# Denominators turned by blocks and inverted by tokens, with a new order of ScalarE's copies and GpSimd's sums, in an mLSTM and gated-unit kernel

## The chip, the core and the metric

The kernel runs on one core of a Trainium2 chip. A core has TensorE (PE: matrix products, with its own queue of weight loads, PEld), VectorE (DVE), ScalarE (ACT), GpSimd (POOL) and SyncE (SP, whose queue starts most transfers). Each engine works through its own list of instructions in order, and they wait for each other by semaphores. The metric is the time of one execution on the device in microseconds (us), lower is better.

## The reference

Two blocks in a row, all in float32, except that `moe_w_in` and `moe_w_out` come as 64-bit floats, which the kernel turns into float32 itself.

```python
# block 1: mLSTM cell, B, H, S, D = 4, 8, 768, 40
for t in range(S):
    m_new = maximum(f_gate[t] + m, i_gate[t])
    f_stab, i_stab = exp(f_gate[t] + m - m_new), exp(i_gate[t] - m_new)
    C = f_stab * C + i_stab * outer(v[t], k[t])      # 40 x 40 for each batch and head
    n = f_stab * n + i_stab * k[t]
    denom = maximum(abs(n . q[t]), 1)
    y[t] = sigmoid(o_gate[t]) * (C @ q[t]) / denom
# block 2: x is (B*S, H*D) = (3072, 320); w_in is 320 x 2048, w_out 2048 x 320
h = x @ w_in
out = (h * cos(h)) @ w_out
```

What matters here is the last line of block 1: every head of every token has one denominator and one output gate for each of its 40 dimensions, and their quotient multiplies the head's vector.

## The kernel before, in words

The 768 tokens of a sequence are cut into six chunks of 128. A *cell* is one chunk of one batch element: cell n = 4c + b is chunk c of batch element b, 24 cells in all. The first four cells (chunk 0) are computed alone in `first_cells`. From then on each step of the program joins two kinds of work: block 2 for chunk c (`Up`, `sums`, `down_slot`) and block 1 for cell n = (c + 1) * 4 + b of the next chunk. `first_parts(b)` does this for c = 0 and `both_parts(c, b)` for c = 1 to 5; in c = 5 there are no cells left. Every such step has two halves, i = 0 and i = 1, and each half makes one pair of 128-wide slices of block 2's hidden layer, f2 = 2b + i.

The order is written out by hand (`tc.manual_schedule()`): the order of calls in the program is the order on each engine. So a call that is moved changes what an engine does first, and what is queued behind an instruction that waits.

**One half of block 2.** `Up` computes `pup` (two PSUM tiles) on TensorE from `xT` and the input weights. `near` (ScalarE) rounds to whole turns, `rest` (VectorE) takes the remainder, `sin` (ScalarE) the sine, `gate` (VectorE) multiplies into `g`. The two `pup` buffers come free when both gates are done. From chunk 1 on the down projection works on 2 x 2 blocks with seven products in place of eight, which needs sums of the gated values (`sums`: four VectorE instructions into `S`, and for c < 5 a GpSimd copy D for later) and sums of the weights (`weight_sums`: four GpSimd instructions, only during c = 0 and 1). TensorE takes those products from `all_products` in portions (`down_slot`, tile `acc`). Two of the seven, `late_products`, run in the next chunk's half f2 = 1. `combine_first`, `combine` and `combine_late` add the parts up to output rows: `m` is a ScalarE copy of an accumulator, `l` a ScalarE copy of the late products, and GpSimd adds `l` to the outputs.

**One cell of block 1.** From chunk 2 on (n >= TWO = 8) a cell is computed in two halves of 64 tokens with the state (`W`, tiles `two`) carried between them. `scores` makes the products of keys and queries and the state's increments, in two `ps` tiles (`pus` is their increment part). `weigh` multiplies by the decays (VectorE, `E<-ps` and `qG<-ps`), `state_half` adds an increment to the state (VectorE, `two<-two,ps`), `keep_end` copies the other increment to `ending` (ScalarE), `fade_end` and `fade_half` scale states (ScalarE, eight copies each), `add_end` adds `ending` to the state (GpSimd, two instructions), `decay_exponents` and `decay` make the next cell's decays (GpSimd, then ScalarE). `turn_blocks` turns the next cell's queries and keys in 32 x 32 blocks (VectorE, tiles `t`), `weigh_k` and `scale_q` weight keys and queries (GpSimd). `values` makes the heads in PSUM tile `vt`, transposed: 32 dimensions and 128 tokens per block of partitions, with the denominator in the row of one of the dimensions. The two `ps` tiles and `vt` share two PSUM buffers.

`turn_gate(n)` turns the output gates (`sig`, tile `og`: by tokens) into the transposed layout (`oT`), and `normalize_turned(n)` normalizes there, all on VectorE, lines 693 to 708: two bounds and a reciprocal over all 128 x 128 elements (of which the rows FROM0 and FROM1 of each block of 32 are denominators), three shuffles that spread them over the block, products with `oT`, and the product into `xT`, the input of block 2. The low dimensions take one more shuffle, one GpSimd product (L709) and two transfers on GpSimd's queue (`low_out`). In chunk 0 of the cells, `normalize` does the same by tokens.

## Time and profile before

| | |
|---|---|
| timed runs | 517.34, 518.75, 519.61 us; median 518.75 |
| the profiled execution | 516.43 us |
| its span, from the first to the last instruction | 514.7 us |
| TensorE's granted clock | 1.000 |
| TensorE busy | 494.4 us, 96% of the span |
| VectorE busy | 422.4 us, 82% |
| ScalarE busy | 350.0 us, 68% |
| GpSimd busy | 236.9 us, 46% |

Busy shares are averages over stages with different limits. A row of the timeline reads: start, duration, engine, source line, operation, output<-inputs, shape, count of merged instructions, and in brackets how long the engine was idle before it and what ended that. A row of a group reads: busy time, mean ns of one, idle time before, and what ended it. In the row of a stretch, each engine has its busy us and its count.

### The profile page before, as it was taken

How to read it: one execution, taken by the hardware profiler on the slowest of the kernel's cores; microseconds unless marked ns; L12 is line 12 of the kernel's file. 1: busy time of each engine (PE TensorE's matmuls, PEld its weight loads, DVE VectorE, ACT ScalarE, POOL GpSimd, SP SyncE). 2: the span in 40 equal slices, each digit the busy share in tenths (PEclk: the TensorE clock that was granted, in tenths of full speed). 3: DMA queues.
4: the chain of work that ended last, by engine and by line, in shares of the span. 5: the costliest groups of instructions: out<-in, count | busy, mean ns of one | idle time of the engine just before them, and what ended most of it. 6: DMA issues, size and time to landing. Idle time of an engine off the chain costs nothing.

```text
span 514.7 us, 12380 instructions
## 1 busy us (share of the span) xinstructions
PE 494.4 (96%) x4567; PEld 329.6 (64%) x4567; DVE 422.4 (82%) x965; ACT 350.0 (68%) x789; POOL 236.9 (46%) x383
## 2 busy tenths in 40 slices
PE   8989899999999999998999998999999999999996
PEld 5764455565565665675676676677676676666756
DVE  6687999987899999979889979889989888564536
ACT  5869897958878778778778787787866541322221
POOL 7626677645686686372462463453462341010000
PEclk9999999999999999999999999999999999999999
DMA  9997999989348156019647008838001000010001
GB/s 136 225 215 208 238 198 271 196 204 201 93 86 167 48 105 121 4 40 214 117 89 139 3 7 212 152 71 156 3 32 52 2 6 6 1 51 2 1 1 51
DMA packets 98092, 53.09 MB, mean 103 GB/s; under 512 B 63344, under 2 KB 90112, under 8 KB 98032
## 3 DMA queue, kind: packets, MB, share of 16 engines
q1 hardware_dynamic: 96176, 50.47, 47.1%
q0 software_dynamic: 1472, 1.48, 1.1%
q8 instruction: 36, 0.59, 0.5%
q10 hardware_dynamic: 384, 0.36, 0.2%
q14 instruction: 24, 0.20, 0.2%
HBM read 46.86 MB, written 4.11 MB: 99 GB/s over the span
## 4 chain that ended last, share of the span: by engine, by line
PE 56%; DVE 23%; ACT 9%; DMA 4%; issue 3%; POOL 3%; SPq 2%; ACTq 0%; DVEq 0%; POOLq 0%
PE pup L848 20%; PE acc L967 17%; PE pup L855 6%; PE po L887 3%; DVE g L875 3%; DVE n L866 3%; PE late L967 2%; PE vt L681 2%; DMA E<-M_d 2%; ACT two L759 2%; DVE E L624 1%; DVE t L563 1%; DVE qG L624 1%; ACT E L496 1%; DVE two L771 1%
## 5 line engine op out<-in xcount | busy, mean ns | idle before, releaser
L848 PE MATMUL pup<-xT,w_in_sb 128*128 128x512 f32 x384 | 176.0, 601 | 3.3 <-DVE g L875 2.5
L848 PEld LDWEIGHTS pup<-xT,w_in_sb 128*128 128x128 f32 x384 | 69.5, 190 | 90.1 <-issue 81.1
L863 ACT ACTIVATE n<-pup 128x512 int32<-128x512 f32 x96 | 53.5, 592 | 89.2 <-PE pup L855 51.4
L866 DVE SCALAR_TENSOR_TENSOR n<-pup,n 128x512 f32<-128x512 f32 x96 | 62.0, 684 | 54.0 <-ACT n L863 53.4
L871 ACT ACTIVATE n<-n 128x512 f32<-128x512 f32 x96 | 58.9, 630 | 25.2 <-DVE n L866 25.2
L759 ACT ACTIVATE two<-two,fades 40x48 f32<-40x48 f32 x224 | 64.0, 326 | 2.1
L875 DVE SCALAR_TENSOR_TENSOR g<-pup,n 128x512 f32<-128x512 f32 x96 | 61.9, 682 | 2.5
L967 PE MATMUL acc<-w_out_sb,g 128*128 128x160 f32 x320 | 58.6, 304 | 0.0
L967 PE MATMUL acc<-T,g 128*128 128x160 f32 x320 | 57.8, 300 | 0.0
L855 PE MATMUL pup<-xT,w_in_l 64*128 64x512 f32 (+1 forms) x256 | 54.0, 628 | 0.0
L967 PEld LDWEIGHTS acc<-w_out_sb,g 128*128 128x128 f32 x320 | 47.8, 190 | 4.7 <-issue 3.9
L967 PEld LDWEIGHTS acc<-T,g 128*128 128x128 f32 x320 | 48.2, 190 | 2.8 <-issue 2.7
L928 POOL COPY D<-S 128x256 f32<-128x256 f32 x32 | 12.7, 397 | 68.7 <-DVE S L924 68.7
L496 ACT ACTIVATE E<-E,tab 128x64 f32<-128x64 f32 (+1 forms) x160 | 42.1, 345 | 0.9 <-POOL E L482 0.7
L887 PE MATMUL po<-w_out_sb,g 128*128 128x320 f32 x128 | 36.4, 437 | 1.2 <-POOL w_out_sb L193 1.2
L967 PE MATMUL acc<-T,S 128*128 128x160 f32 x160 | 34.9, 300 | 0.0
L709 POOL TENSOR_TENSOR oT<-oT,db 128x128 f32<-128x128 f32 x16 | 7.3, 457 | 58.3 <-DVE oT L708 58.3
L887 PEld LDWEIGHTS po<-w_out_sb,g 128*128 128x128 f32 x128 | 23.7, 190 | 12.1 <-POOL w_out_sb L193 1.6
L482 POOL TENSOR_SCALAR_AFFINE_SELECT E<-E 64x512 f32<-64x512 f32 (+1 forms) x38 | 28.1, 740 | 4.0 <-DVE E L479 1.8
L967 PE MATMUL acc<-w_out_sb,S 128*128 128x160 f32 x160 | 28.7, 299 | 0.0
L855 PEld LDWEIGHTS pup<-xT,w_in_l 64*128 64x128 f32 (+1 forms) x256 | 13.3, 158 | 23.8 <-issue 19.5
L967 PEld LDWEIGHTS acc<-T,S 128*128 128x128 f32 x160 | 26.3, 190 | 2.7 <-issue 2.7
(234 smaller groups left out, 906.7 us busy)
## 6 DMA issues: line engine op xcount, KB each, us to landing
qr<-in_q_dram SPq DMA_DIRECT2D x36, 160.0 KB
G<-G_d SPq DMA_DIRECT2D x20, 256.0 KB
bits<-in_moe_w_out_dram SPq DMA_DIRECT2D x8, 640.0 KB
kr<-in_k_dram SPq DMA_DIRECT2D x32, 160.0 KB
bits<-in_moe_w_in_dram SPq DMA_DIRECT2D x32, 128.0 KB
E<-M_d SPq DMA_DIRECT2D x32, 128.0 KB
out_dram<-o_sb SPq DMA_DIRECT2D x22, 160.0 KB
o<-in_o_gate_dram SPq DMA_DIRECT2D x40, 80.0 KB
```

The source lines that it names most:

```text
L482: nc.gpsimd.affine_select(out=E[x:x + w], in_=E[x:x + w], compare_op=OP.is_ge, fill=1.0e30, base=0, pattern=[[0, H], [1, w]], channel_mult ...
L496: nc.scalar.activation(out=Es[n][:, h], in_=Es[n][:, h], func=AF.Exp, scale=-1.0, bias=tab[:, c, 0, g:g + 1])
L759: nc.scalar.activation(out=dst[rows(o, D), x:x + DV], in_=src[rows(i, D), x:x + DV], func=AF.Copy, scale=fades[rows(j, D), k, g:g + 1])
L848: nc.tensor.matmul(pu, w_in_sb[:, i, ts(2 * f2 + e, 128)], x(i), start=(i == 0 and not low_first), stop=(i == NK - 1 and low_first))
L855: nc.tensor.matmul(pu[y:y + w], w_in_l[r, f2, y:y + w], x(NK, r), start=low_first, stop=not low_first)
L863: nc.scalar.activation(out=self.n[e], in_=self.pu[e], func=AF.Copy, bias=0.25)
L866: nc.vector.scalar_tensor_tensor(out=self.n[e].bitcast(FP), in0=self.pu[e], scalar=0.25, in1=self.n[e], op0=OP.add, op1=OP.subtract)
L871: nc.scalar.activation(out=r, in_=r, func=AF.Sin, scale=TWO_PI_DOWN)
L875: nc.vector.scalar_tensor_tensor(out=g, in0=self.pu[e], scalar=TWO_PI, in1=self.n[e].bitcast(FP), op0=OP.mult, op1=OP.mult)
L887: nc.tensor.matmul(po[c][b], gs[c, f][:, ts(b, C)], w_out_sb[:, f], start=(f == 0), stop=(f == NF - 1))
L928: nc.gpsimd.tensor_copy(out=Ds[c, k // 4][:, k % 4], in_=S[:, 1, 0:3:2])
L967: nc.tensor.matmul(a, lhs, rhs, start=start, stop=stop)
```

## The change

Three things change; TensorE's instructions stay, in the same order.

1. `turn_gate` is gone. `normalize_turned` now first turns the block rows that hold the denominators from PSUM with one block transpose, so that they lie by tokens; bounds and inverts only the 8 columns that are denominators (4 blocks of tokens, 2 heads); multiplies them into the gates `og` in place (two products); turns the gates; and multiplies the heads with them from PSUM directly into `xT` (one product for n >= TWO, two before) and `yt`. The shuffles that spread the denominators, the products before them, and GpSimd's product (L709) are gone.
2. `keep_end` stands before `rest`, so ScalarE's `ending` copies come before the sines. In odd halves `fade_end` and `fade_half` stand behind `sums` and behind `combine` and the late products; ScalarE's copies m and l thus come before the sixteen scaled copies.
3. On GpSimd `weight_sums` stands behind `sums`, `add_end` before `scale_q`, and the sums of the late products (`add_late`) behind `scale_q`.

```diff
-    def turn_gate(n):
-        c, b = divmod(n, B)
-        oTs[n] = p1.tile([128, 3, C], FP, name="oT", tag="oT")
-        nc.vector.transpose(out=oTs[n].rearrange("q g (t k) -> q g k t", t=32), in_=sig[c][:, b].rearrange("q (g k) i -> q g k i", g=3))
...
     def normalize_turned(n):
         c, b = divmod(n, B)
-        dn = p1.tile([128, C], FP, name="dt", tag="dt")
-        yt = p1.tile([128, 3, C], FP, name="yt", tag="yt")
         va, vb = heads_of[n]
-        parts = [(yt[:, 0:3:2], va, oTs[n][:, 0:3:2]), (yt[:, 1], vb, oTs[n][:, 1])]
-        nc.vector.tensor_scalar(out=dn, in0=va[:, 1], scalar1=-TWO_PI, scalar2=TWO_PI, op0=OP.mult, op1=OP.max)
-        nc.vector.scalar_tensor_tensor(out=dn, in0=va[:, 1], scalar=TWO_PI, in1=dn, op0=OP.mult, op1=OP.max)
-        for o, v, g in parts:
-            nc.vector.tensor_tensor(out=o, in0=v, in1=g, op=OP.mult)
+        K = C // 32
+        dt = p1.tile([128, K, 32], FP, name="dt", tag="dt")
+        nc.vector.transpose(out=dt, in_=va[:, 1].rearrange("q (t k) -> q k t", t=32))
+        dn = p2.tile([128, K, 2], FP, name="dn", tag="dn")
+        both = dt[:, :, FROM0:FROM1 + 1:FROM1 - FROM0]
+        nc.vector.tensor_scalar(out=dn, in0=both, scalar1=-TWO_PI, scalar2=TWO_PI, op0=OP.mult, op1=OP.max)
+        nc.vector.scalar_tensor_tensor(out=dn, in0=both, scalar=TWO_PI, in1=dn, op0=OP.mult, op1=OP.max)
         nc.vector.reciprocal(out=dn, in_=dn)
-        db = p1.tile([128, 3, C], FP, name="db", tag="db")
-        for i, mask in enumerate(([FROM0] * 32, [FROM1] * 32, [FROM0] * 16 + [FROM1] * 16)):
-            nc.vector.stream_shuffle(out=db[:, i], in_=dn, mask=mask)
+        o = sig[c][:, b]
+        whole = o[:, 0:2 * K].rearrange("q (g k) i -> q g k i", g=2)
+        nc.vector.tensor_tensor(out=whole, in0=whole, in1=dn.rearrange("q k g -> q g k").unsqueeze(3).to_broadcast([128, 2, K, 32]), op=OP.mult)
+        mixed = o[:, 2 * K:3 * K].rearrange("q k (g i) -> q k g i", g=2)
+        nc.vector.tensor_tensor(out=mixed, in0=mixed, in1=dn.unsqueeze(3).to_broadcast([128, K, 2, 16]), op=OP.mult)
+        oT = p1.tile([128, 3, C], FP, name="oT", tag="oT")
+        nc.vector.transpose(out=oT.rearrange("q g (t k) -> q g k t", t=32), in_=o.rearrange("q (g k) i -> q g k i", g=3))
...
-        nc.vector.tensor_tensor(out=xT[c][:, 0:NK, b], in0=yt[:, 0:NK], in1=db[:, 0:NK], op=OP.mult)
-        y = yt[:, NK]
+        yt = p1.tile([128, 3, C], FP, name="yt", tag="yt")
+        nc.vector.tensor_tensor(out=yt[:, 0], in0=va[:, 1], in1=oT[:, NK], op=OP.mult)
+        ys[n] = yt[:, 0]
         if n >= TWO:
-            y = oTs[n][:, NK]
-            nc.vector.stream_shuffle(out=y, in_=yt[:, NK], mask=[16 * (i // 16) + i % 16 // 2 + 8 * (i % 2) for i in range(32)])
-        nc.gpsimd.tensor_tensor(out=y, in0=y, in1=db[:, NK], op=OP.mult)
-        ys[n] = y
+            nc.vector.stream_shuffle(out=yt[:, 1], in_=yt[:, 0], mask=[16 * (i // 16) + i % 16 // 2 + 8 * (i % 2) for i in range(32)])
+            ys[n] = yt[:, 1]
+        if n >= TWO:
+            nc.vector.tensor_tensor(out=xT[c][:, 0:NK, b], in0=whole_z[n], in1=oT[:, 0:NK], op=OP.mult)
+        else:
+            nc.vector.tensor_tensor(out=xT[c][:, 0, b], in0=va[:, 0], in1=oT[:, 0], op=OP.mult)
+            nc.vector.tensor_tensor(out=xT[c][:, 1, b], in0=vb, in1=oT[:, 1], op=OP.mult)
...
     # combine_late: the GpSimd sums of l and their transfers move to a function of their own
+    def add_late(c):
+        o, t = outs_of[c, 1], late[c]
         for e, i in ((0, 0), (1, 0), (0, 1)):
             nc.gpsimd.tensor_tensor(out=o[e][:, HALF:DM], in0=t[:, i], in1=o[e][:, HALF:DM], op=OP.add)
...
     # both_parts(c, b)
             for e in range(2):
                 up.near(e)
+            if cell and i == 0:
+                keep_end(n)
             for e in range(2):
                 up.rest(e)
             if i == 0:
...
-                if c == 1 and b > 0:
-                    weight_sums(f2)
                 for e in range(2):
                     up.sin(e)
                     up.gate(e)
-                if cell:
-                    keep_end(n)
                 if c > 1 and f2 > 1:
                     down_slot(c, f2)
                 sums(c, f2)
+                if c == 1 and b > 0:
+                    weight_sums(f2)
...
             else:
                 if cell and n + 1 < N:
                     weigh_k(n + 1)
-                if c == 1:
-                    weight_sums(f2)
                 for e in range(2):
                     up.sin(e)
                     up.gate(e)
-                if cell:
-                    fade_end(n)
-                    if n + 1 < N:
-                        fade_half(n + 1)
                 if c > 1 and f2 > 1:
                     down_slot(c, f2)
                 sums(c, f2)
...
+                if c > 1 and f2 == 1:
+                    for p in (1, 0):
+                        combine(c - 1, p)
+                    down_slot(c, f2)
+                if cell:
+                    fade_end(n)
+                    if n + 1 < N:
+                        fade_half(n + 1)
+                if c == 1:
+                    weight_sums(f2)
+                if cell:
+                    add_end(n)
                 if cell and n + 1 < N:
                     odd_values(n + 1)
             if f2 == 1 and c > 1:
                 if cell:
                     scale_q(n + 1)
-                for p in (1, 0):
-                    combine(c - 1, p)
-            if c == 1 and f2 > 0 or c > 1 and f2 < 2:
+                add_late(c - 1)
+            if c == 1 and f2 > 0 or c > 1 and f2 == 0:
                 down_slot(c, f2)
             if cell and i == 0:
-                turn_gate(n)
                 values(n)
...
                 if cell:
-                    add_end(n)
                     if n % 2 == 1 and n + 3 < N:
                         load_two(n + 3, "Kv")
```

More of the change, by code (lines that the diff above doesn't have):

```diff
@@ L683, in values_of_halves @@
         heads_of[n] = z[:, 0:3:2], z[:, 1]
+        whole_z[n] = z[:, 0:NK]
+    whole_z = {}
     FROM0, FROM1 = 0, 16
@@ L1020, in combine_late @@
             return
-        t = p1.tile([128, 3 * C], FP, name="l", tag="oT")[:, 0:DM].rearrange("q (h n) -> q h n", h=2)
+        t = late[c] = p1.tile([128, 3 * C], FP, name="l", tag="oT")[:, 0:DM].rearrange("q (h n) -> q h n", h=2)
         nc.scalar.copy(out=t, in_=L)
+    def add_late(c):
+        o, t = outs_of[c, 1], late[c]
         for e, i in ((0, 0), (1, 0), (0, 1)):
@@ L1408, in both_parts @@
                     scale_q(n + 1)
-                for p in (1, 0):
-                    combine(c - 1, p)
-            if c == 1 and f2 > 0 or c > 1 and f2 < 2:
+                add_late(c - 1)
+            if c == 1 and f2 > 0 or c > 1 and f2 == 0:
                 down_slot(c, f2)
             if cell and i == 0:
-                turn_gate(n)
                 values(n)
```

## The prediction

> **What bounds the kernel now.** I read the page's first line, then the busy time by stretch. The stretches are the first cells (before 58.6 us, not shown), the first up-projection chunk c = 0, and then the chunks c = 1 to 4. Columns after the stretch: its length, then busy us and count for PE, PEld, DVE, ACT and POOL.
>
> ```profile
> span 514.7 us, 12380 instructions
> 58.60:135.50 76.90, 75.01 (x540) 42.75 (x544) 67.29 (x143) 61.96 (x122) 49.03 (x71) 1.00 0.95 202
> 135.50:211.00 75.50, 72.28 (x817) 47.53 (x816) 72.52 (x158) 59.46 (x150) 54.64 (x88) 1.00 0.50 102
> 211.00:290.00 79.00, 75.86 (x856) 52.31 (x860) 69.04 (x167) 62.28 (x156) 36.58 (x59) 1.00 0.49 98
> 290.00:367.00 77.00, 74.86 (x828) 51.55 (x828) 66.72 (x163) 62.09 (x154) 35.96 (x59) 1.00 0.50 100
> 367.00:444.00 77.00, 77.00 (x743) 52.79 (x743) 65.65 (x164) 41.72 (x96) 25.86 (x43) 1.00 0.05 17
> ```
>
> TensorE has no gap in c = 4: there only its own work counts. In c = 1 to 3 it idles 3.2 + 3.1 + 2.1 = 8.5 us, and the change doesn't touch its instructions or their order, so 8.5 us is all that can be won there. The view of waits, for TensorE between 135.5 and 367 us, names the whole of it; the timeline then gives the places.
>
> ```profile
> PE vt L681 <- ACT ending L776: 5.2, 4, 1.7
> PE ps L604 <- DVE t L563: 2.5, 4, 0.6
> PE pup L848 <- DVE g L875: 0.8, 2, 0.4
> ```
> ```profile
> 168.39 0.69 PE L604 MATMUL ps<-t,t 40*64 40x64 f32 x32 [0.64 <-DVE t L563]
> 187.13 0.69 PE L604 MATMUL ps<-t,t 40*64 40x64 f32 x32 [0.64 <-DVE t L563]
> 211.47 0.65 PE L681 MATMUL vt<-E,two 128*32 128x64 f32 x32 [1.15 <-ACT ending L776]
> 222.00 3.70 PE L848 MATMUL pup<-xT,w_in_sb 128*128 128x512 f32 x8 [0.40 <-DVE g L875]
> 233.35 0.65 PE L681 MATMUL vt<-E,two 128*32 128x64 f32 x32 [1.74 <-ACT ending L776]
> 289.89 0.65 PE L681 MATMUL vt<-E,two 128*32 128x64 f32 x32 [0.54 <-ACT ending L776]
> 300.43 3.70 PE L848 MATMUL pup<-xT,w_in_sb 128*128 128x512 f32 x8 [0.40 <-DVE g L875]
> 311.79 0.65 PE L681 MATMUL vt<-E,two 128*32 128x64 f32 x32 [1.74 <-ACT ending L776]
> ```
>
> So c = 1 loses 0.64 in each of four cells (2.5 us), and c = 2 and c = 3 lose it only in their first two cells: 1.15 + 0.40 + 1.74 = 3.3 and 0.54 + 0.40 + 1.74 = 2.7 us.
>
> **c = 1: VectorE, and what slows it.** A cell there lasts 187.13 - 168.39 = 18.74 us, of which TensorE needs 18.1. One VectorE cell of c = 3, and the one wait in a cell of c = 1:
>
> ```profile
> 326.57 1.29 DVE L866 SCALAR_TENSOR_TENSOR n<-pup,n 128x512 f32<-128x512 f32 x2 [1.86 <-ACT n L863]
> 327.89 0.86 DVE L624 TENSOR_TENSOR E<-ps,E 64x256 f32<-64x256 f32 x2
> ...
> 333.08 0.87 DVE L568 STREAM_TRANSPOSE oT<-og 128x384 f32<-128x384 f32 x1
> ...
> 336.98 1.27 DVE L866 SCALAR_TENSOR_TENSOR n<-pup,n 128x512 f32<-128x512 f32 x2
> ...
> 341.54 1.10 DVE L563 STREAM_TRANSPOSE t<-qr 128x512 f32<-128x512 f32 x1
> ...
> 345.42 1.29 DVE L866 SCALAR_TENSOR_TENSOR n<-pup,n 128x512 f32<-128x512 f32 x2 [1.85 <-ACT n L863]
> 168.49 1.29 DVE L866 SCALAR_TENSOR_TENSOR n<-pup,n 128x512 f32<-128x512 f32 x2 [0.25 <-ACT n L863]
> ```
>
> The c = 3 cell holds 345.42 - 326.57 - 1.85 = 17.0 us of work; the same instructions take 18.74 - 0.25 = 18.5 us in c = 1. The difference is in the four sums of `sums`, beside which GpSimd runs `weight_sums`. The same group between 150 and 205 us, then between 320 and 350 us:
>
> ```profile
> L922 DVE TENSOR_TENSOR g<-g 128x256 f32<-128x256 f32 x6 | 3.8, 629 | 0.2
> L922 DVE TENSOR_TENSOR g<-g 128x256 f32<-128x256 f32 x3 | 1.3, 425 | 0.1
> ```
>
> 629 ns against 425. The change puts `weight_sums` behind `sums` on GpSimd in both halves of a cell, so these 1.5 us (18.5 - 17.0) go. In odd halves the weight sums then lie beside the q and k transposes, in even ones beside the new normalization, whose two gate products, like those sums, read two SBUF tensors; the old one had a single such product, away from the weight sums. So the gate products can lose what L922 loses, 2 x 0.2 us. [...]
>
> **The normalization.** Now it takes 336.98 - 333.08 = 3.90 us. Prices for the new one:
>
> ```profile
> L717 DVE SCALAR_TENSOR_TENSOR dn<-ph,least 128x8 f32<-128x8 f32 x4 | 0.6, 161 | 2.3 <-PE ph L641 2.3
> ...
> L719 DVE RECIPROCAL dn<-dn 128x8 f32<-128x8 f32 x4 | 0.8, 204 | 0.1
> L568 DVE STREAM_TRANSPOSE oT<-og 128x384 f32<-128x384 f32 x20 | 17.5, 876 | 2.6 <-ACT og L385 2.6
> ```
>
> Two bounds (0.16 each, from L717) and a reciprocal on 8 columns: 0.53. A product over 256 columns: 0.43, twice (gates, xT); over 128 columns, between 0.16 and 0.43, 0.29 by proportion, for the mixed gates, yt and the shuffle. The gate transpose stays, 0.88. The transpose of the denominators has no row: 0.29 if it cost as a product of its size, 0.88 if no less than the one three times as wide; I take 0.40, proportion to L568 above a fixed 0.16. Sum: 0.53 + 0.86 + 0.87 + 0.88 + 0.40 = 3.5 us, with no overlap counted since nearly every step waits for the one before. That is 0.4 less, with bounds of -0.5 and +0.5. [...] No run here shows a transpose from PSUM.
>
> VectorE per cell of c = 1, with the 0.4 that the gate products may lose: 18.5 - 1.5 - 0.4 + 0.4 = 17.0, a us below TensorE's 18.1. The transposes t then end before TensorE asks, and the 0.64 goes.
>
> The new wait lies here. The `ending` copies now stand before the sines, so the products E<-ps on VectorE, on the same banks, wait for them; the copies wait for GpSimd's `add_end` of the cell before (it frees `ending`), which stands behind D and four weight sums. Behind the copies are queued the sines, and behind E<-ps the gates.
>
> ```profile
> 182.67 0.72 POOL L911 TENSOR_TENSOR T<-w_out_sb 128x160 f32<-128x160 f32 x1
> ...
> 185.34 0.39 POOL L928 COPY D<-S 128x256 f32<-128x256 f32 x1
> 170.60 1.25 POOL L787 TENSOR_TENSOR two<-two,ending 40x192 f32<-40x192 f32 x2
> 211.10 0.65 ACT L776 COPY ending<-ps 40x192 f32<-40x192 f32 x2 [1.74 <-DVE two L771]
> ```
>
> Round the loop: E<-ps to the end of the second sums 341.54 - 327.89 = 13.65, less 0.4 for the normalization; D 0.5 with its start; weight sums 185.34 - 182.67 = 2.7; `add_end` 1.25; one copy 0.35; less 0.4 because only the second E<-ps waits for the last copy. That is 17.65 us, and 18.05 if the gate products are slowed: just below 18.1. I leave 0.3 us in c = 1 for it. Gain 2.2.
>
> **c = 2 and c = 3, first two cells.** At 233.35 the cause is ScalarE's order:
>
> ```profile
> 221.85 4.78 ACT L759 ACTIVATE two<-two,fades 40x48 f32<-40x48 f32 x16
> 226.53 0.27 ACT L980 COPY m<-acc 128x160 f32<-128x160 f32 x1
> ...
> 227.02 1.07 ACT L863 ACTIVATE n<-pup 128x512 int32<-128x512 f32 x2
> ```
> ```profile
> 226.83 0.49 DVE L981 TENSOR_TENSOR o_sb<-acc,m 128x320 f32<-128x320 f32 x1 [2.50 <-ACT m L980]
> ...
> 229.31 1.28 DVE L866 SCALAR_TENSOR_TENSOR n<-pup,n 128x512 f32<-128x512 f32 x2
> ```
>
> Sixteen scaled copies stand before m; VectorE waits 2.50 for m, then does seven output sums, so its rest (229.31) starts 2.3 us after ScalarE's rounding (227.02). With m and l first, the output sums fill the 2.5 us of idle, the rounding stays at about 227.0 (l waits for `late`, which ends before 222.0), and rest follows after one rounding, 0.6 us: 1.7 earlier. That ends the 1.74. The sixteen copies keep their cover, TensorE's next `pup`.
>
> At 211.47 and 289.89 vt waits for the `ending` copy that follows VectorE's state sums; with the copy made earlier vt waits for those sums alone, one copy (0.3 to 0.4) sooner, and VectorE comes there 0.4 us earlier by the normalization, at 211.47 also by the odd half's part of the 1.5, some 0.7. 0.54 goes; of 1.15 I leave 0.2. At 222.00 and 300.43 the gate is late behind ScalarE's sigmoid, which started only after `ending`; both come forward by the above, over 0.40. Leaving 0.4 in c = 2 (another 0.2 for the moved GpSimd work) and 0.3 in c = 3: gains 2.9 and 2.4.
>
> **c = 0.** Only the normalization changes, four times, and GpSimd loses one product. Of the 1.9 us that TensorE idles there, the chain of waits runs through a transfer:
>
> ```profile
> 52.86 5.40 DMA bits<-in_moe_w_out_dram
> ```
>
> What VectorE wins before 58.3 us ends in that landing; later its products meet GpSimd's weight conversion. I count 0, bounds +0.8 (four times 0.2 of contention) and -1.6 (four times 0.4).
>
> **Sum.** 2.2 + 2.9 + 2.4 = 7.5 us. The profiled execution took 516.43 us (span 514.7 and 1.7 around it), so 508.9; it is 2.3 below the median of the timed runs, 518.75, and against that the forecast is 511.2 us.
>
> **Rivals.**
> First: the loop through `add_end` holds c = 1 at today's 18.74 us. For it: 18.05 is a sum with 0.05 us to spare, and spans on GpSimd are rough. Then 2.2 is lost: 513.4.
> Second: the change doesn't do what it says at the seams, because the rounding comes later behind l and the scaled copies than I think. If rest stays at its present place in both seams, 1.74 comes back twice, and with the first rival's loss the gain is 7.5 - 3.5 - 2.2 = 1.8: 517.0. Against it: VectorE's 2.50 wait names m alone.
> Third, slower: VectorE's two gate products are not slowed but held through the whole run of weight sums. The trace has a hold:
>
> ```profile
> 358.93 0.42 DVE L921 TENSOR_TENSOR S<-g 128x256 f32<-128x256 f32 x1 [0.46 <-POOL kw L500]
> ```
>
> Held for 2.7 us, the loop is 18.05 + 2.7 = 20.7; four cells cost 2.0 more each than today, 8.0, less 5.3 won at the seams: 521.5. It decides from a hold of 2.0 us on (4 x 1.3 = 5.3); the sums in the same place were only stretched by half.
>
> **How the numbers follow.** Forecast 0.65 (its own range 508.9 to 513.0: all 8.5 won and 1.3 of c = 0, or 1.8 less won), first rival 0.17, second 0.10, third 0.08. A measurement of this kernel tells about 0.5%, 2.6 us. Faster by more: 0.65 + 0.17 = 0.82; within: 0.10; slower: 0.08. The range 508.8 to 515.6 takes in the first case, the first rival and, with c = 0's +0.8 and a seam wait kept, 2.2 above it; the other two are left out.
>
> **What would show it.** In the changed profile, TensorE's waits for t (L563) and for `ending` should be nearly gone between 135 and 360 us; its idle there about 1 us instead of 8.5; L922's group 425 ns in c = 1; the normalization 3.5 us, and the wait for m near 0. The forecast is wrong if E<-ps waits for `ending` by more than 0.5 us per cell of c = 1, or if the first rounding after the late products starts over a us after TensorE's `pup`.

## The result, and the profile after

Six timed runs of each kernel, side by side: 517.17 us before, 511.48 us after (medians), ratio 0.989 with a 95% interval of 0.986 to 0.993. The change makes the kernel 1.1% faster, by 5.7 us where the sum said 7.5. The forecast of 511.2 us was set against the median of 518.75 of the runs shown; as a ratio it was 0.985. That 511.48 lies so near to 511.2 is luck in part: the kernel before was itself 1.6 us faster in these runs than in those.

The page's first line and first busy figures of the changed kernel, and its busy time by stretch: the stretches run from the first product `vt` beside one chunk c to the first beside the next (c = 0 counted from TensorE's wait at 58 us). Columns as in the prediction.

```profile
span 509.6 us, 12299 instructions
PE 495.3 (97%) x4567; PEld 331.7 (65%) x4567; DVE 411.8 (81%) x889; ACT 350.2 (69%) x789; POOL 224.8 (44%) x363
58.10:136.16 78.06, 74.75 (x536) 42.77 (x536) 67.01 (x134) 62.93 (x124) 47.55 (x68) 1.00 0.96 202
136.16:210.78 74.62, 72.75 (x817) 48.79 (x817) 68.00 (x141) 60.32 (x151) 48.68 (x82) 1.00 0.50 99
210.78:286.81 76.03, 76.03 (x849) 52.74 (x849) 65.68 (x150) 61.72 (x154) 36.14 (x58) 1.00 0.52 102
286.81:362.74 75.93, 75.93 (x834) 52.73 (x833) 65.63 (x150) 61.84 (x154) 34.72 (x55) 1.00 0.51 102
362.74:438.95 76.21, 76.21 (x738) 52.22 (x738) 62.16 (x146) 41.18 (x95) 23.47 (x38) 1.00 0.05 17
```

The waits of TensorE between 135.5 and 362.7 us, the whole view:

```profile
PE pup L853 <- DVE g L880: 1.4, 3, 0.5
PE vt L676 <- DVE two L776: 0.4, 1, 0.4
```

The waits for t and for `ending` are gone; 8.5 us of idle became 1.9. But in c = 1 a new wait, for the gates, stands in their place. And the three chunks together did not become 6.6 us shorter but 5.7: TensorE's busy time in them rose by 0.9 us with the same instructions. The timeline shows the main place: rows of four merged products of `pup`, one of the kernel before, then the same of the changed one.

```profile
155.13 1.13 PE L855 MATMUL pup<-xT,w_in_l 64*128 64x512 f32 x4
154.89 1.49 PE L860 MATMUL pup<-xT,w_in_l 64*128 64x512 f32 x4
```

Each of the four still takes 0.59 to 0.69 us, but the second and the fourth start 0.36 us later behind the first, because they write the buffer that the second gate frees (that gate ends at 155.20, the second product starts at 155.26). Meanwhile the first product still counts as running, so this wait is counted as busy.

Chunk lengths, from first `vt` to first `vt`, are therefore the measure used below. The start of c = 1 is not: over the fourteen profiles of the table it lies between 134.8 and 136.9 us, and is up to 1.8 us apart for kernels that are the same up to there, so whole spans compare to within a us or two only. Chunk lengths repeat far better: c = 2 lasts 76.02 or 76.03 us in the four kernels that are the same there (the changed one, weights_in_odd, bounds_from_psum and old_norm_early).

| kernel | start of c = 1 | c = 1 | c = 2 | c = 3 | ratio to before, 95% interval |
|---|---|---|---|---|---|
| before | 135.44 | 76.03 | 78.42 | 77.83 | |
| changed | 136.16 | 74.62 | 76.03 | 75.93 | 0.989 (0.986 to 0.993) |
| norm_alone | 136.20 | 75.33 | 78.47 | 77.85 | 1.000 (0.998 to 1.002) |
| order_alone | 136.55 | 73.62 | 76.48 | 76.38 | 0.989 (0.987 to 0.991) |
| fades_first | 136.93 | 74.68 | 76.49 | 76.38 | 0.993 (0.990 to 0.995) |
| ending_late | 135.73 | 75.43 | 77.11 | 76.42 | 0.994 (0.992 to 0.996) |
| weights_in_odd | 136.19 | 74.21 | 76.02 | 75.93 | 0.990 (0.987 to 0.993) |
| m_early | 136.15 | 74.70 | 75.61 | 75.53 | 0.988 (0.986 to 0.991) |
| bounds_from_psum | 135.12 | 74.86 | 76.02 | 75.93 | 0.988 (0.985 to 0.992) |
| old_norm_early | 134.80 | 73.63 | 76.02 | 75.93 | 0.989 (0.986 to 0.992) |
| weights_back | 136.56 | 75.52 | 76.47 | 76.38 | 0.993 (0.991 to 0.996) |
| best | 135.13 | 73.64 | 75.61 | 75.51 | 0.987 (0.985 to 0.990) |
| best_odd_ahead | 135.19 | 73.90 | 75.61 | 75.51 | 0.988 (0.985 to 0.991) |
| turn_first | 135.72 | 73.22 | 75.61 | 75.52 | 0.984 (0.981 to 0.987) |

**A cell of c = 1 in the changed kernel** (VectorE, with one of GpSimd's weight sums, ScalarE's first rounding and TensorE's `pup`, in order of time):

```profile
157.17 0.31 DVE L690 STREAM_TRANSPOSE dt<-vt 128x128 f32<-128x128 f32 x1
157.51 0.29 DVE L693 TENSOR_SCALAR dn<-dt 128x8 f32<-128x8 f32 x1
157.84 0.45 DVE L694 SCALAR_TENSOR_TENSOR dn<-dt,dn 128x8 f32<-128x8 f32 x1
...
158.35 0.53 POOL L917 TENSOR_TENSOR w_out_sb<-w_out_sb 128x160 f32<-128x160 f32 x1
158.56 0.59 DVE L698 TENSOR_TENSOR og<-og,dn 128x256 f32<-128x256 f32 x1
159.08 0.62 DVE L700 TENSOR_TENSOR og<-og,dn 128x128 f32<-128x128 f32 x1
...
161.51 1.28 DVE L871 SCALAR_TENSOR_TENSOR n<-pup,n 128x512 f32<-128x512 f32 x2
162.89 1.29 DVE L880 SCALAR_TENSOR_TENSOR g<-pup,n 128x512 f32<-128x512 f32 x2
...
163.64 3.70 PE L853 MATMUL pup<-xT,w_in_sb 128*128 128x512 f32 x8 [0.37 <-DVE g L880]
168.47 1.09 ACT L868 ACTIVATE n<-pup 128x512 int32<-128x512 f32 x2 [0.18 <-PE pup L860]
169.10 1.29 DVE L871 SCALAR_TENSOR_TENSOR n<-pup,n 128x512 f32<-128x512 f32 x2 [1.15 <-ACT n L868]
```

The normalization runs from 157.17 to 161.51, 4.34 us instead of 3.5. Then a chain goes round: odd gate (162.89), TensorE's `pup` on the buffers that the gates free (163.64), ScalarE's rounding (168.47), VectorE's rest of the even half (169.10), for which VectorE idles 1.15 us. From odd gate to even rest it is 6.21 us. In the trace of before it was 6.21 too: the prediction's own rows have the rest at 168.49, and this is the odd gate of that cell:

```profile
162.28 1.29 DVE L875 SCALAR_TENSOR_TENSOR g<-pup,n 128x512 f32<-128x512 f32 x2
```

### The profile page after: what moved, and what is told of

The parts are those of the page before. It is cut to its first block, busy times and chain, and to the rows that moved or that the text cites. A ratio compares the mean times of both kernels' runs of the same rounds, so it can differ in the third digit from the quotient of the medians.

```text
span 509.6 us, 12299 instructions
## 1 busy us (share of the span) xinstructions
PE 495.3 (97%) x4567; PEld 331.7 (65%) x4567; DVE 411.8 (81%) x889; ACT 350.2 (69%) x789; POOL 224.8 (44%) x363
## 3 DMA queue, kind: packets, MB, share of 16 engines
q0 software_dynamic: 1472, 1.48, 1.1%
## 4 chain that ended last, share of the span: by engine, by line
PE 76%; DVE 14%; ACT 3%; POOL 2%; issue 2%; SPq 1%; DMA 1%; DVEq 0%; POOLq 0%; ACTq 0%
PE pup L853 27%; PE acc L972 22%; PE pup L860 8%; PE po L892 4%; PE late L972 4%; PE vt L676 3%; DVE n L871 2%; DVE g L880 2%; PE ph L636 1%; DMA bits<-in_moe_w_out_dram 1%; PE ps L611 1%; PE ps L599 1%; ACT E L496 1%; PE ps L604 1%; SPq L170 1%
## 5 line engine op out<-in xcount | busy, mean ns | idle before, releaser
L860 PE MATMUL pup<-xT,w_in_l 64*128 64x512 f32 (+1 forms) x256 | 56.5, 628 | 0.1
L818 POOL DMA_DIRECT2D xT<-yt x40 | 22.0, 551 | 53.2 <-DVE yt L709 31.2
L860 PEld LDWEIGHTS pup<-xT,w_in_l 64*128 64x128 f32 (+1 forms) x256 | 15.3, 158 | 24.4 <-issue 20.2
L482 POOL TENSOR_SCALAR_AFFINE_SELECT E<-E 64x512 f32<-64x512 f32 (+1 forms) x38 | 27.9, 735 | 3.6 <-DVE E L479 1.8
```

Source lines behind the costliest of these rows:

```text
L482: nc.gpsimd.affine_select(out=E[x:x + w], in_=E[x:x + w], compare_op=OP.is_ge, fill=1.0e30, base=0, pattern=[[0, H], [1, w]], channel_mult ...
L818: nc.gpsimd.dma_start(out=xT[c][64 * e:64 * e + 64, NK, b], in_=ys[n][1:128:2])
L860: nc.tensor.matmul(pu[y:y + w], w_in_l[r, f2, y:y + w], x(NK, r), start=low_first, stop=not low_first)
```

## Experiments

All kernels differ from the changed one, or from the one before, by the edits shown. "Theory 1" in the expectations is the loop just read; "theory 2" is the prediction's sum of VectorE's work.

**norm_alone: the new normalization in the old order.** Edit: of the diff, `normalize_turned`, `whole_z` and the missing `turn_gate` alone.

> The kernel before with the new normalization alone, its old order kept. Theory 1 (a loop sets chunk 1): from the second gate of an odd half through TensorE's next pup, the rounding, and VectorE's work up to the next such gate. The changed kernel's cells of chunk 1 last 18.7 to 18.85 us, hardly less than the 18.73 of before, because its normalization takes 4.4 us there beside the weight sums instead of 3.6. With the weight sums in their old place it should take 3.6 against 3.8 to 4.0, so the cell falls by some 0.3 us: 1.2 us in chunk 1, about as much at the seams of chunks 2 and 3, less some 0.7 us lost in chunk 0: 1.5 to 2 us faster than before. Theory 2 (the prediction's: VectorE's whole work per cell counts, and the weight sums beside the sums are what costs): 0.4 us in each of four cells and nothing lost in chunk 0, 1.6 us and 0.7 us more at the seams: 2.3 us. Rival: the normalization is hidden and alone moves nothing, or loses 0.7 us in chunk 0.

Ratio 1.000: the rival was right, the normalization alone moves nothing. In the profile the 0.7 us that c = 1 wins are lost ahead of it (start at 136.20 instead of 135.44). The cell of c = 1 did fall, as theory 1 said (18.73 to 18.51 in each of two cells; c = 1 from 76.03 to 75.33), but at the seams nothing came: TensorE waits 5.2 us for `ending` as before. The length of the normalization was not what `vt` waited for there; whether it was the place of ScalarE's copies, fades_first and ending_late test.

**order_alone: parts 2 and 3 with the old normalization.**

Edit: `turn_gate` and `normalize_turned` of the kernel before, everything else of the change.

> The changed kernel with the old normalization (turn_gate, shuffles, GpSimd's product) put back: parts 2 and 3 alone. Theory 1: the seams of chunks 2 and 3 keep nearly all they won (2.4 + 1.9 us in the changed trace), chunk 1 wins 0.3 us a cell from sums that are no longer slowed, and chunk 0's loss of 1.4 us does not come: about 5.5 us faster than before, as fast as the changed kernel (within 1 us). Theory 2: the normalization's 0.4 us a cell is missing, chunk 1 still falls to TensorE's own 18.1 us: 6.0 to 6.5 us faster than before. Rival: the new normalization is what wins, and without it less than 3 us is left.

As fast as the changed kernel: in sum the whole gain is the order. In c = 1 it is a us better without the new normalization (73.62 against 74.62), in c = 2 and c = 3 0.45 us worse in each. VectorE's odd gate, even rest and next odd gate:

```profile
163.19 1.29 DVE L878 SCALAR_TENSOR_TENSOR g<-pup,n 128x512 f32<-128x512 f32 x2
169.40 1.29 DVE L869 SCALAR_TENSOR_TENSOR n<-pup,n 128x512 f32<-128x512 f32 x2 [0.97 <-ACT n L866]
181.52 1.29 DVE L878 SCALAR_TENSOR_TENSOR g<-pup,n 128x512 f32<-128x512 f32 x2
```

Again 6.21 us; then 12.12 on VectorE, a cell of 18.33. In the changed kernel the second part is 12.64, in the kernel before 12.53.

**fades_first: the sixteen scaled copies back behind the gates.**

```diff
                 for e in range(2):
                     up.sin(e)
                     up.gate(e)
+                if cell:
+                    fade_end(n)
+                    if n + 1 < N:
+                        fade_half(n + 1)
...
-                if cell:
-                    fade_end(n)
-                    if n + 1 < N:
-                        fade_half(n + 1)
```

> The changed kernel with the sixteen scaled copies (fade_end, fade_half) back behind the gates, ahead of the sums, of m and of l. If the wait of 2.50 us for m was what made the rest late at the seams, the waits of about 1.7 us in the first cells of chunks 2 and 3 come back: 3.3 to 4 us slower than the changed kernel, VectorE idle by about 2 us for m again. Rival: VectorE's rest waits for the rounding anyway, which stands behind the sixteen copies in both kernels (VectorE is idle 2.06 us for it in the changed kernel); then it costs 1.5 us at most.

0.46 us in each of c = 2 and c = 3, near the rival. VectorE does wait for m again, but `vt` hardly does:

```profile
226.01 0.49 DVE L986 TENSOR_TENSOR o_sb<-acc,m 128x320 f32<-128x320 f32 x1 [2.54 <-ACT m L985]
231.84 0.66 PE L676 MATMUL vt<-E,two 128*32 128x64 f32 x32 [0.36 <-DVE two L776]
```

Counted from TensorE's second `pup` (222.00 before, 222.04 here), the state sums are done 0.84 us earlier than before (the copies themselves start 0.9 us earlier, since all that precedes them does), and `vt` follows those sums 0.7 us closer, since the `ending` copy is no longer behind them. So without the early m and l, other parts of the change still take most of the 1.74.

**ending_late: `keep_end` back behind the gates.**

```diff
-            if cell and i == 0:
-                keep_end(n)
...
                     up.gate(e)
+                if cell:
+                    keep_end(n)
```

> The changed kernel with ScalarE's ending copies back behind the gates. If they matter by themselves, vt waits for the last copy again at the first cells of chunks 2 and 3, by 0.3 to 0.4 us each, three or four times: 0.7 to 1.4 us slower than the changed kernel, nothing in chunk 1. Rival 1: with m early VectorE's state sums end in time and the copies too, so nothing changes (within 0.3 us). Rival 2: without the copies ahead of E<-ps the loop through GpSimd's add_end opens and chunk 1 gains up to 0.3 us a cell, 1 us faster.

2.4 us over the three chunks (0.8, 1.1, 0.5), more than any theory gave. `vt` waits at the seams, the rows below, where the changed kernel has 0.44 and then nothing; in c = 1 the first cell takes 18.39 instead of 17.70, and in c = 2 the last cell takes 18.94 instead of 18.25.

```profile
211.16 0.65 PE L676 MATMUL vt<-E,two 128*32 128x64 f32 x32 [1.23 <-ACT ending L781]
231.45 0.65 PE L676 MATMUL vt<-E,two 128*32 128x64 f32 x32 [0.28 <-ACT ending L781]
288.27 0.65 PE L676 MATMUL vt<-E,two 128*32 128x64 f32 x32 [0.63 <-ACT ending L781]
```

Of the 4.3 us that c = 2 and c = 3 won, undoing the copies' place costs 1.6, undoing the place of the scaled copies 0.9, and undoing the normalization 0.9. Where the remaining 0.9 comes from is not shown: parts of the change that can stand in for each other would leave such a rest, but no run undoes the places of `add_end` and `add_late` either.

**weights_in_odd: no weight sums beside the normalization.**

```diff
                 if cell and n + 1 < N:
                     weigh_k(n + 1)
+                if c == 1:
+                    weight_sums(f2)
...
-                if c == 1 and b > 0:
-                    weight_sums(f2)
...
-                if c == 1:
-                    weight_sums(f2)
                 if cell:
                     add_end(n)
+                if c == 1 and f2 < LAST:
+                    weight_sums(f2 + 1)
```

> The changed kernel with chunk 1's weight sums all in odd halves: those of f2 behind weigh_k, ahead of the sums, and those of f2 + 1 behind add_end; none beside the normalization. Theory 1 (the loop): in the kernel before, the changed one, the new normalization alone and the new order alone, the time from an odd half's first gate to the next even half's first rest is the same 6.21 us (162.28 to 168.49, 162.89 to 169.10, 162.94 to 169.15, 163.19 to 169.40), and the cell of chunk 1 is 6.21 plus VectorE's work from that rest to the next odd half's first gate: 12.52, 12.63, 12.30, 12.12, for cells of 18.73, 18.84, 18.51, 18.33. Taking the weight sums off the normalization (4.4 to 3.6) shortens that part to 11.8 and the cell to 18.0 or TensorE's own 17.7 to 18.1, although the odd half's sums are slowed again: three cells by 0.7 to 0.8, 2.0 to 2.4 us faster than the changed kernel. Theory 2 (VectorE's whole work per cell): the same contention is only moved, from products and bounds to sums, so nothing changes (within 0.5 us). Rival: GpSimd's add_end comes too late behind the longer run and holds the ending copies; then it is slower.

The normalization fell to 3.5 us, but the cell only to 18.4: c = 1 is 0.4 us shorter, as theory 2 said, though not for its reason. GpSimd's masks for the decays (L482) moved back by a us, onto the even sums:

```profile
155.26 1.45 POOL L482 TENSOR_SCALAR_AFFINE_SELECT E<-E 64x512 f32<-64x512 f32 x2
155.34 0.86 DVE L926 TENSOR_TENSOR S<-g 128x256 f32<-128x256 f32 x1
156.23 0.76 DVE L927 TENSOR_TENSOR g<-g 128x256 f32<-128x256 f32 x1
168.46 0.69 PE L599 MATMUL ps<-t,t 40*64 40x64 f32 x32 [0.27 <-DVE t L563]
```

0.86 and 0.76 where the changed kernel has 0.69 and 0.42 (in the next cell 0.78 and 0.76 for 0.86 and 0.43), and the slowed odd sums now make t late. What was not on the path came onto it when the loop became shorter.

**m_early: m in a buffer of its own, fade_end between m and l.**

```diff
-        s = p1.tile([128, 3 * C], FP, name="m", tag="yt" if p else "db")
+        s = p1.tile([128, 3 * C], FP, name="m", tag="db")
...
                         combine(c - 1, p)
-                    down_slot(c, f2)
                 if cell:
                     fade_end(n)
+                if c > 1 and f2 == 1:
+                    down_slot(c, f2)
+                if cell:
                     if n + 1 < N:
                         fade_half(n + 1)
```

> The changed kernel with m's tile in a buffer of its own (in the changed kernel it shares the buffer of yt and so waits 1.07 us for the transfers of the low dimensions), and with fade_end's eight copies between m and l, so that ScalarE isn't idle until the late products end. The sixteen scaled copies then end 0.7 to 0.9 us earlier, the first rounding of the even half follows TensorE's pup (225.8 us in the changed trace) instead of the copies (226.57), and rest, E<-ps and the gates come 0.7 earlier. If that is what holds the second cell of chunks 2 and 3 (19.20 us against 18.8 for the others, its low pup products at 1.54 us instead of 1.13): 0.4 us in each of two chunks, 0.8 us faster than the changed kernel. Rival: the gates wait for something else there, nothing changes.

As expected: the second cells of c = 2 and c = 3 fall from 19.20 to 18.79, 0.4 us in each. What held them in the changed kernel (ScalarE, then VectorE's rest):

```profile
221.21 0.29 ACT L985 COPY m<-acc 128x160 f32<-128x160 f32 x1 [1.07 <-DMA xT<-yt]
221.86 4.81 ACT L764 ACTIVATE two<-two,fades 40x48 f32<-40x48 f32 x16
226.57 1.05 ACT L868 ACTIVATE n<-pup 128x512 int32<-128x512 f32 x2
227.18 1.29 DVE L871 SCALAR_TENSOR_TENSOR n<-pup,n 128x512 f32<-128x512 f32 x2 [2.06 <-ACT n L868]
```

m shares a buffer with `yt`, from which the change lets the transfers of the low dimensions read (before they read `oT`); so m waits for them. That wait alone doesn't explain the 0.4, though. Behind m stands l, which needs the late products, and these end at 221.37; l starts at 221.41. By these times, with m earlier and nothing else moved, the sixteen copies would still stand behind an l that starts there. The run takes both away at once: m is done early, and eight of the copies fill ScalarE's time until l can start. Neither edit was run alone.

**bounds_from_psum: the two bounds ahead of the turn, for the cells beside c = 0 and 1.**

```diff
+        early = n < 3 * B
...
+        if early:
...
+            nc.vector.tensor_scalar(out=turned, in0=va[:, 1], scalar1=-TWO_PI, scalar2=TWO_PI, op0=OP.mult, op1=OP.max)
+            nc.vector.scalar_tensor_tensor(out=turned, in0=va[:, 1], scalar=TWO_PI, in1=turned, op0=OP.mult, op1=OP.max)
+        nc.vector.transpose(out=dt, in_=turned.rearrange("q (t k) -> q k t", t=32))
...
+        nc.vector.reciprocal(out=dn, in_=both if early else dn)
```

> The changed kernel with, for the cells of chunks 1 and 2 (worked beside c = 0 and 1), the two bounds taken over all 128 columns from PSUM, ahead of the turn, as the old normalization did, and only the reciprocal on 8 columns behind it. In the changed kernel the bounds on 8 columns, both operands in SBUF, take 1.47 and 0.53 us beside GpSimd's weight conversion (they end when its instruction ends), against 0.17 each alone; the old ones from PSUM took 0.27 and 0.29 in the same place. If the place of the operand decides: the normalization in c = 0 falls from 4.9 to about 3.8 us, the cell that begins at 93 us from 22.1 to 21.55 as in the kernels with the old normalization, and chunk 1's cells by 0.1 to 0.2: 0.7 to 1.2 us faster than the changed kernel. Rival: the transposes or the reciprocal are held in their place, since the GpSimd instruction still runs; then nothing is won in c = 0.

The same place in the changed kernel, beside GpSimd's weight conversion, and then here:

```profile
95.53 1.57 POOL L193 TENSOR_TENSOR w_out_sb<-w_out_sb,bits 128x640 int32<-128x640 int32 x1 [1.88 <-ACT E L496]
95.65 1.48 DVE L693 TENSOR_SCALAR dn<-dt 128x8 f32<-128x8 f32 x1
97.05 0.62 POOL L752 TENSOR_TENSOR S<-S,fades 128x256 f32<-128x256 f32 x1
97.16 0.53 DVE L694 SCALAR_TENSOR_TENSOR dn<-dt,dn 128x8 f32<-128x8 f32 x1
```
```profile
94.81 0.28 DVE L694 TENSOR_SCALAR db<-vt 128x128 f32<-128x128 f32 x1
95.12 0.29 DVE L695 SCALAR_TENSOR_TENSOR db<-vt,db 128x128 f32<-128x128 f32 x1
95.02 1.57 POOL L193 TENSOR_TENSOR w_out_sb<-w_out_sb,bits 128x640 int32<-128x640 int32 x1 [1.87 <-ACT E L496]
115.12 1.58 POOL L193 TENSOR_TENSOR w_out_sb<-w_out_sb,bits 128x640 int32<-128x640 int32 x1 [3.10 <-DMA qr<-in_q_dram]
115.85 0.29 DVE L694 TENSOR_SCALAR db<-vt 128x128 f32<-128x128 f32 x1 [0.97 <-PE pu L665]
```

Eight columns from SBUF take 1.48 us, until GpSimd's instruction ends (95.53 + 1.57 = 97.10, against 97.13); sixteen times as many from PSUM take 0.28 and 0.29. The first bound at 94.81 is nearly done when the conversion starts; the one at 95.12, and the pair of the next cell from 115.85, run wholly beside it and are no longer for it. The cell from 93 us falls from 22.10 to 21.55, as with the old normalization, and the one ahead of it from 23.03 to 22.49. In c = 1 nothing was won (74.86 against 74.62): the bounds take 0.57 from PSUM in place of 0.74, but the turn takes 0.41 from SBUF in place of 0.31. Why the bounds from PSUM are not held, no run shows: the place of their source and the number of columns changed together.

**old_norm_early: the old normalization beside c = 0 and 1, the new one from c = 2 on.** Edit: `if n < 3 * B` chooses the old `turn_gate` and `normalize_turned`.

> The changed kernel with the old normalization for the cells worked beside c = 0 and 1, and the new one from c = 2 on. By the stages of the runs so far it should have chunk 1 of the new order alone (73.6 against 74.6 us), the cell at 93 us of the old normalization (21.55 against 22.1), and chunks 2 and 3 of the changed kernel (76.0 and 75.9 against 76.5 and 76.4): 1.5 us faster than the changed kernel. Rival: the stages are not additive, since an earlier chunk 1 meets other waits; then 0.5 us or nothing.

The stages add up as told: 73.63, 76.02, 75.93, and 21.56 for the cell at 93 us; the span is 507.2, 2.4 less than the changed kernel's: 1.0 in c = 1, 0.5 in the cell at 93 us, and 0.8 ahead of that, in the part that scatters. The timed runs scatter too much to show 1.5 us (509.6 to 513.8).

**weights_back: order_alone with GpSimd's weight sums in their old places.** Edit: both `weight_sums` calls as before the change.

> The new order alone (old normalization), with GpSimd's weight sums back in their old places: behind the decay exponents in even halves, behind weigh_k in odd ones. So the ending copies, m, l and add_end keep the new order; the weight sums again run beside VectorE's sums. Theory 1 (the loop of 6.21 us and VectorE's part from the even rest to the odd gate): the even sums take 2.4 to 2.5 us as in the kernel before instead of 2.0, so the cells of chunk 1 go from 18.3 to 18.7, 1.2 us slower than the new order alone over three cells; the odd half's slowed sums cost nothing. Theory 2 (the prediction: all 1.5 us of slowed sums count): back to 18.74 in every cell and TensorE's waits of 0.64 for t, 2 us slower. Rival: chunk 1's gain came from the ending copies and add_end; then no change (within 0.4 us).

Cells of 18.7 in place of 18.3, as theory 1 gave (12.52 after 6.21), and TensorE's waits of 0.55 for t back, as theory 2 gave; with the first cell, c = 1 loses 1.9 us. So moving the weight sums won 1.9 of the 2.4 us by which c = 1 of order_alone is shorter than before.

```profile
163.60 1.29 DVE L878 SCALAR_TENSOR_TENSOR g<-pup,n 128x512 f32<-128x512 f32 x2
169.81 1.29 DVE L869 SCALAR_TENSOR_TENSOR n<-pup,n 128x512 f32<-128x512 f32 x2 [0.22 <-ACT n L866]
182.33 1.29 DVE L878 SCALAR_TENSOR_TENSOR g<-pup,n 128x512 f32<-128x512 f32 x2
```

**best and best_odd_ahead: old_norm_early with m_early's edit; then also the odd half's weight sums ahead of the sums again.**

> The changed kernel with the old normalization for the cells worked beside c = 0 and 1, m in a buffer of its own and fade_end's copies between m and l: the stages that won in single runs, together. If they add up as the stages of the traces do (2.4 us and 0.6 us of span): span 506.4 to 506.6 us, 9 us below the kernel before's 514.7 less its own scatter, 1.6% faster than before. Rival: old normalization's shuffles write the buffer that m now uses, and m or the shuffles wait for each other; then nothing is won over the old normalization early.

> The same, with the odd half's weight sums back behind weigh_k, ahead of the sums (as before), and the even half's still behind the sums. Theory 1: the odd sums are slowed by 0.6 us, where VectorE waits 0.97 us for the rounding anyway, so that costs nothing; add_end, scale_q and the decay exponents come 2 us earlier on GpSimd, so the even sums lose their slowing beside the exponents (0.43 + 0.75 us instead of twice 0.43) and the second ending copy its wait of 0.26: cells of chunk 1 at 17.9 to 18.1 instead of 18.3, 0.6 to 1.0 us faster than the kernel beside it. Theory 2: VectorE's whole work is what counts, and 0.6 us more of it in four cells makes it 1 to 2 us slower.

The first adds up in the stages (73.64, 75.61, 75.51; span 506.8). The second is a miss of theory 1: one cell falls to 17.97, as it gave, but the next lasts 18.46 and the first 18.77, with TensorE waiting 0.45 and 0.57 for t behind slowed odd sums. c = 1 is 0.26 us longer.

**turn_first: best_odd_ahead with the transposes t ahead of the odd sums.**

```diff
+                if c == 1 and cell:
+                    turn_blocks(n + 1)
                 sums(c, f2)
...
-                    turn_blocks(n + 1)
+                    if c > 1:
+                        turn_blocks(n + 1)
```

> The kernel best_odd_ahead with, in chunk 1's odd halves, the block transposes t ahead of the four sums on VectorE. In best_odd_ahead one cell lasts 17.97 us, what the loop gives with free even sums, and the next 18.46, where TensorE waits 0.6 us for t behind the slowed odd sums. With t first that wait goes, the weight sums fall beside the transposes, and the sums still end ahead of the rounding. If the loop of 6.21 us plus VectorE's part (11.8) is then all that holds chunk 1: cells of 17.9 to 18.1, chunk 1 in 72.5 to 73.0 us instead of 73.9, 1 us faster than best_odd_ahead and best. Rival: D, behind the later sums, holds add_end and the ending copies; then chunk 1 stays at 73.5 to 74.

c = 1 takes 73.22 us, in cells of 17.96, 18.19, 18.19 and 18.88; no wait for t. Short of the 72.5 to 73.0 expected, in part because the first even sum still meets GpSimd's masks (0.63 us instead of 0.43). At 0.984 (0.981 to 0.987) it has the lowest ratio of the study; its interval and the changed kernel's meet only at their ends, but it overlaps those of best and best_odd_ahead.

```profile
162.21 1.29 DVE L912 SCALAR_TENSOR_TENSOR g<-pup,n 128x512 f32<-128x512 f32 x2
168.42 1.29 DVE L903 SCALAR_TENSOR_TENSOR n<-pup,n 128x512 f32<-128x512 f32 x2 [1.06 <-ACT n L900]
180.40 1.29 DVE L912 SCALAR_TENSOR_TENSOR g<-pup,n 128x512 f32<-128x512 f32 x2
```

## Why the prediction was right, and where it was not

The direction, the stages and the bound on what can be won (TensorE's own idle) held. Of 7.5 us, 5.1 came in the span: 1.4 in c = 1 (2.2 forecast), 2.4 in c = 2 (2.9), 1.9 in c = 3 (2.4), 0.1 behind, and 0.7 lost ahead of c = 1, inside the bound of 0.8 but also inside that part's scatter.

- **c = 1, mis-sized by the wrong sum.** The step "VectorE per cell of c = 1 ... 17.0, a us below TensorE's 18.1. The transposes t then end before TensorE asks, and the 0.64 goes" failed. The wait for t went, but the cells stayed at 18.69 and 18.85. The row that the prediction quoted for the kernel before had the answer: VectorE's rest at 168.49 waits 0.25 for the rounding, so VectorE's work between odd gate and even rest was not full, and what is saved there (the odd sums, t) cannot count. Only the part from even rest to odd gate does, and there the change took 0.3 to 0.5 off the even sums and put 0.4 on the normalization. The 1.4 us that came are from the first and last cell (18.65 to 17.70, 19.92 to 19.38). The first cell goes back to 18.39 with the `ending` copies late (ending_late) and from 18.04 to 18.76 with the weight sums back (weights_back against order_alone), so both bear on it; the last was not taken apart. Nor is 18.1 what TensorE needs: best_odd_ahead and turn_first have cells of 17.97 and 17.96, so at least 0.1 us of the 18.74 less the visible wait of 0.64 was not its own work.
- **Contention.** L922's group fell to 425 ns in c = 1, as forecast (L927 now). Its price on the gate products was set at 0.2 each; the groups of c = 1, then the same of c = 3, show 0.17 and 0.32. The two bounds, which the prediction priced without contention, lose 0.12 and 0.28 besides: 0.29 and 0.45 in c = 1 against 0.17 alone.

```profile
L927 DVE TENSOR_TENSOR g<-g 128x256 f32<-128x256 f32 x6 | 2.5, 425 | 0.2
L700 DVE TENSOR_TENSOR og<-og,dn 128x128 f32<-128x128 f32 x3 | 1.8, 609 | 0.0
L698 DVE TENSOR_TENSOR og<-og,dn 128x256 f32<-128x256 f32 x3 | 1.8, 592 | 0.1
L698 DVE TENSOR_TENSOR og<-og,dn 128x256 f32<-128x256 f32 x2 | 0.8, 425 | 0.1
L700 DVE TENSOR_TENSOR og<-og,dn 128x128 f32<-128x128 f32 x2 | 0.6, 284 | 0.0
```

- **The normalization.** 3.5 us forecast; 3.6 from c = 2 on, with the transposition at 0.31 where 0.40 was taken, and 4.3 in c = 1. In bounds_from_psum the same transposition took 0.41 us from SBUF and 0.31 from PSUM. The old normalization beside the moved weight sums still takes 3.90 us (order_alone, 157.91 to 161.81).
- **The seams.** "That ends the 1.74" came true, but not by m and l first alone, to which that step gave it: undoing this brings back 0.36 of the wait and costs 0.46 a chunk. The `ending` copies, put at 0.3 to 0.4 in one place, are worth 1.1 and 0.5, the normalization 0.45 in each. What stayed, 0.4 in each second cell, came from the sixteen copies standing behind both m and l: l can't start before the late products end, and m meanwhile waited for a transfer that the prediction did not look for, since the changed kernel's buffers were read for contents, not for who still reads them. m_early took both away.
- **c = 0.** Counted at nothing with 0.8 of contention as a bound. Two cells lose 0.55 and about 0.3 us (the second of these is within what that cell scatters by). The cause of the first is a hold as in the third rival, on another operation and in another stage than it was put: the bounds, 1.48 us beside the weight conversion and 0.53 beside the product that follows it on GpSimd, against 0.17 each alone.
- **Rivals.** The first named the right outcome for c = 1's ordinary cells, with the wrong loop: `add_end` held the second `ending` copy only in kernels with the old normalization (order_alone, old_norm_early, best), by 0.25 to 0.28 us. The second did not come: rest starts 2.1 us earlier at the seam, 1.4 us counted from the chunk's first `vt`, where the step gave 1.7. Nor did the third, a hold of the gate products through a whole run of weight sums. But its contrast was wrong: the sums that it calls stretched were held too, each for the rest of the one GpSimd instruction that ran when it started, and so were the gate products (the numbers are in the last section). Its 4 x 1.3 is 5.2, not 5.3. Among the signs named, E<-ps waits for no copy, and the rounding starts 0.75 us behind `pup`, under the us that was set.

## What to carry to other kernels

When an engine and TensorE feed each other through two buffers, follow one round of the loop and see on which arc the engine waits: work saved on the arc where it already idles, even for 0.25 us, is worth nothing, and the engine's total of work says nothing about it. Before an order is changed, ask of each instruction that is moved what it will now run beside, and of each buffer that is given a new use who still reads the old. Undo each part alone: costs of undoing need not add up to the gain, and the largest part of an edit, here the normalization, can be worth nothing in sum: 0.45 us won in each of two chunks, a us lost in a third.

## What was not expected of the hardware

- In the changed kernel a VectorE bound on 8 columns (TENSOR_SCALAR, or SCALAR_TENSOR_TENSOR with both sources in SBUF) was held until the running GpSimd instruction ended: 1.48 us beside a 1.57 us conversion of 32-bit integers (from 95.65), against 0.17 alone (215.02). Up to the end of c = 1, every one that started beside a GpSimd instruction ended 0.02 to 0.03 us after it. A reciprocal on 8 columns kept its 0.20 us beside the conversion (bounds_from_psum, 95.90), and beside a GpSimd product that ended 0.32 us after it (changed kernel, 50.58). With the source in PSUM and 128 columns, TENSOR_SCALAR took 0.29 us beside the conversion (bounds_from_psum, 115.85). Larger two-source products in SBUF look only stretched in their groups' means (for the products into `og` 592 ns against 425 for 256 columns and 609 against 284 for 128, beside the weight sums and without them), but they were held in the same way: in c = 1 of the changed kernel each product into `og` that starts beside a weight sum ends 0.27 us (256 columns) or 0.14 to 0.16 us (128 columns) after it (159.15 against 158.88 for the first). In c = 1 of the kernel before, each sum that starts 0.13 us or more behind the start of a GpSimd instruction that still runs ends 0.27 to 0.30 us after that instruction, while two that start within 0.01 us of one keep their 0.42 us (135.70 and 173.38). So what contention cost in these rows was the rest of one GpSimd instruction, not a ratio.
- A block transpose of 128 x 128 took 0.31 us from PSUM (changed kernel, 157.17) and 0.41 from SBUF (bounds_from_psum).
